# Input read in the transform's own layout, its scale moved into the convolution's kernel, and an inverse stage in eight groups

## The chip, the cores and the metric

The kernel runs on one core of a Trainium2 chip. It has the engines PE (matmul; its weight loads are listed as PEld), DVE, ACT and POOL, and SP, which only issues DMAs here. The metric is the device time of one execution in microseconds; smaller is better. Shares and single durations come from one profiled execution, the times from separate runs.

## The reference

One block of a conditioned state-space layer: a layer norm with shift and scale from a condition vector, a long convolution per channel, a gate and a residual; then a second norm and a two-layer feed-forward part with a squared ReLU. L = 2048 tokens, D = 512 channels, N = 128 states per channel, F = 1792.

```
mod = silu(c) @ w_mod                       # sa, ca, ga, sb, cb, gb, 512 each
h = layernorm(x) * (1 + ca) + sa
K[d, l] = Re sum_n C[d,n] * exp(dt[d] * A[d,n] * l) * dt[d] * B[d,n]
x = x + ga * (causal_conv(h, K) + h * Dskip)
h = layernorm(x) * (1 + cb) + sb
x = x + gb * (relu(h @ w1 + b1)**2 @ w2 + b2)
```

## The kernel before

The convolution is done by a transform of length 2048, split as 32 x 64 (a token is 64 a + b, with b permuted and counted by j), on eight chunks of 64 channels, c = 0 to 7. Partitions hold 32 values of a for each of four groups of 128 channels; along a partition run j and the channels.

**Start.** `parameters` works out the phases and amplitudes of all states from A, B, C and dt on DVE, ACT and POOL, first for chunk 0, then for the other seven. The input x arrives as 16 row blocks `rows` of 128 tokens by 512 channels. For each, DVE takes mean and variance (L527, L528), subtracts the mean and multiplies by the scale (L597), multiplies by the reciprocal deviation and adds the shift (L598); 16 matmuls with columns of the identity turn the block into the transform's layout (L602) and ACT copies it into `big1` (L605). Scale and shift rows `g1`, `s1` come from matmuls of the condition with `w_mod` (L550, L587).

**Main loop**, 32 units u of 16 channels, four to a chunk. For each unit POOL makes phases (`kgen_phase`, L729) and amplitudes (`kgen_amp`, L749, L753), ACT their sine, absolute value and cosine (`kgen_sin`, L739 to L741), DVE the products (`kgen_rl`, L763 to L766), and PE sums over the states into a PSUM bank `kg` (`kgen_mm`, L773); copied to `ksb` (L836), that is a piece of the convolution kernel K. Both K and the input go through `stage1` (L639, copy L641) and `stage2` (L649). For the input the result is kept by ACT (L672), and two DMAs make a copy with its halves exchanged (L676); for the kernel, DVE multiplies stage two's result with both (L783). A matmul back (L792) and two DVE copies (L798) leave each chunk in `big0` and `big1`. Which chunk's pieces are issued behind which unit is written by hand in the string `ORDER`: capitals are the input's pieces (`u_pieces`), small letters the products (`product_pieces`), `x` exponentials (L720), `l` the late modulation, `r` the row pieces. Seven large tiles `xy` are handed round for all of this; one buffer of them holds a stationary operand's source until its last reader is done.

**Inverse stage.** `inverse(n)`, n = 0 to 3, each 128 matmuls of 32x32 by 128 columns (L946), gives four blocks s of 128 tokens each in the four halves of the PSUM tiles `tg`; n = 0 is added to x by DVE (L953), the others are copied by ACT (L955) and added by POOL (L958). `statistics` and `prepare` normalize (L964 to L973), transpose (L979), apply scale and shift (L982, L986) and split each block into a high half (L990, ACT) and a low half (L992, POOL) of reduced-precision numbers. The weights w1 and w2 are split likewise (L897, L918 for w1; `split`, L893, L894, for w2). L975 adds the gated bias b2 to x.

**Feed-forward.** For each of four groups of 512 tokens 14 tiles: `ffn1` (L1040, L1041 on the high half, L1043 on the low) and, two tiles later, `ffn2` (L1060 to L1062).

**What sets the order.** The program is traced, and `keep_order` then lists it anew for every engine: a list scheduler with a cost for each instruction (`weight`), a model of PE's clock, the dependences, and a priority that is the cost to the end plus a number given by `hurry` for single passages. Groups in `in_turn` keep the order of the source. SP's DMAs go by the source's order as they become ready. Each engine then runs its list strictly in order.

## Time and profile before

| | us |
|---|---|
| runs, without the profiler | 654.75, 654.25, 648.11 (median 654.25) |
| the profiled execution's own time | 646.92 |
| its span, first to last instruction | 645.1 |
| start, until stage one of the input begins (L639) | 63.5 |
| main loop, until the first inverse matmul (L946) | 232.1 |
| inverse stage, until ffn2 begins | about 40 |
| feed-forward, from there to the end | about 309 |

The parts are cut at the first instruction named. PE's clock column shows 1.00 of full speed except in the inverse stage, where stretches of 16 us show between 0.68 and 0.89. A line of a group gives busy time, the mean of one instruction and the idle time of its engine before it with what ended it; a matmul in this number format appears as two records.

### The profile page before, as it was taken

The numbers are of one execution on the slowest core, as the hardware profiler recorded it, in microseconds if no ns is written. First come the engines' busy times: TensorE is split into PE (matmuls) and PEld (weight loads), VectorE is DVE, ScalarE is ACT, GpSimd is POOL, SyncE is SP. The second block draws the span as 40 slices with busy tenths as digits, with TensorE's granted clock in tenths as the row PEclk, the third lists the DMA queues.
The fourth block names the chain that finished last, engine by engine and source line by source line (L and its number), as shares of the span: only waits on it lengthen the run. The fifth ranks groups of instructions, "written<-read, shape, count | busy, mean of one in ns | idle before, by whom it ended". The sixth has DMA issues, their size and how long they took to land.

```text
span 645.1 us, 20810 instructions
## 1 busy us (share of the span) xinstructions
PE 584.7 (91%) x9314; PEld 507.1 (79%) x9314; DVE 384.0 (60%) x655; ACT 342.2 (53%) x632; POOL 302.7 (47%) x243
## 2 busy tenths in 40 slices
PE   1367998999899999987899999999999999999995
PEld 1265997899799998885668888888888888888884
DVE  6999956899799778744659532533325333252223
ACT  5963888989887977361645532244322433222220
POOL 5696799889999887158969300011000100000000
PEclk9999999999999999998799999999999999999998
DMA  9942030311331233465222000100001000010001
GB/s 324 381 133 68 3 69 4 68 36 38 69 70 39 82 69 86 139 206 201 85 83 73 28 0 1 65 1 0 1 1 66 1 1 1 0 66 0 1 1 65
DMA packets 21705, 42.30 MB, mean 66 GB/s; under 512 B 3696, under 2 KB 9200, under 8 KB 20336
## 3 DMA queue, kind: packets, MB, share of 16 engines
q1 hardware_dynamic: 21184, 40.84, 20.8%
q8 instruction: 73, 1.20, 0.8%
q10 hardware_dynamic: 432, 0.14, 0.1%
q14 instruction: 16, 0.13, 0.1%
HBM read 28.39 MB, written 4.19 MB: 51 GB/s over the span
## 4 chain that ended last, share of the span: by engine, by line
PE 71%; DVE 11%; POOL 7%; issue 5%; ACT 4%; DMA 2%; DVEq 0%; SPq 0%; POOLq 0%; ACTq 0%
PE tg L1060 8%; PE tg L1062 8%; PE tg L1061 8%; PE ps L1040 6%; PE ps L1041 6%; PE ps L1043 6%; PE ps L649 6%; PE ps L792 6%; PE ps L639 5%; PE kg L773 3%; PE kg L1040 2%; PE kg L1041 2%; PE kg L1043 2%; ACT tables L720 2%; DVE xy L598 2%
## 5 line engine op out<-in xcount | busy, mean ns | idle before, releaser
L1048 DVE TENSOR_TENSOR xy<-xy 128x512 f32<-128x512 f32 x56 | 44.6, 796 | 157.8 <-ACT rw L1047 106.2
L1046 ACT ACTIVATE xy<-ps,b1c 128x512 f32<-128x512 f32 x42 | 28.9, 688 | 129.7 <-PE ps L1043 129.7
L975 POOL TENSOR_TENSOR big<-big,lo 128x512 f32<-128x512 f32 x16 | 21.6, 1355 | 152.9 <-DVE xy L973 152.5
L649 PE MATMUL ps<-xy,t_sb 128*64 128x64 f32 x2048 | 67.1, 223 | 1.8 <-DVE xy L783 0.9
L649 PEld LDWEIGHTS ps<-xy,t_sb 128*64 128x64 f32 x2048 | 63.9, 138 | 3.8 <-issue 1.1
L792 PE MATMUL ps<-e_sb,xy 128*64 128x128 f32 x1024 | 61.3, 274 | 4.7 <-ACT xy L641 1.9
L792 PEld LDWEIGHTS ps<-e_sb,xy 128*64 128x64 f32 x1024 | 56.0, 139 | 6.3 <-ACT xy L641 2.3
L641 ACT COPY xy<-ps 128x512 f32<-128x512 f32 x64 | 36.8, 589 | 11.8 <-PE ps L639 10.1
L753 POOL TENSOR_TENSOR rtl<-tables 128x1024 f32<-128x1024 f32 x22 | 43.0, 1955 | 0.1
L783 DVE TENSOR_TENSOR xy<-ps,xy 128x512 f32<-128x512 f32 x64 | 40.0, 683 | 2.0 <-PE ps L649 1.7
L798 DVE COPY big<-ps 128x256 f32<-128x256 f32 x64 | 24.2, 419 | 20.3 <-PE ps L792 20.0
L729 POOL TENSOR_TENSOR llph<-lo,big 128x1024 int32<-128x1024 int32 x16 | 34.3, 2141 | 3.8 <-ACT tg L741 2.3
L1040 PE MATMUL ps<-h0h,w1h 128*128 128x512 f32 x88 | 35.8, 407 | 0.0
L729 POOL TENSOR_TENSOR rtl<-lo,big 128x1024 int32<-128x1024 int32 x16 | 34.3, 2141 | 2.8 <-ACT tg L741 2.1
L639 PE MATMUL ps<-d_sb,ksb 128*64 128x128 f32 x512 | 33.2, 274 | 1.1 <-DVE ksb L837 0.6
L639 PE MATMUL ps<-d_sb,big 128*64 128x128 f32 x512 | 31.4, 274 | 0.8 <-ACT big L605 0.7
L1040 PE MATMUL ps<-h,w1h 128*128 128x512 f32 x80 | 31.4, 393 | 0.0
L1046 ACT ACTIVATE xy<-kg,b1c 128x512 f32<-128x512 f32 x14 | 9.6, 689 | 39.4 <-PE kg L1043 39.4
L1049 DVE TENSOR_TENSOR rw<-xy,rw 128x512 fp32r<-128x512 f32 x37 | 28.5, 770 | 2.9
L639 PEld LDWEIGHTS ps<-d_sb,ksb 128*64 128x64 f32 x512 | 28.0, 137 | 2.3 <-DVE ksb L837 1.0
L639 PEld LDWEIGHTS ps<-d_sb,big 128*64 128x64 f32 x512 | 27.9, 137 | 2.0 <-ACT big L605 1.0
L773 PE MATMUL kg<-rtl 128*32 128x64 f32 x1408 | 25.6, 221 | 4.1 <-issue 4.1
(247 smaller groups left out, 1574.0 us busy)
## 6 DMA issues: line engine op xcount, KB each, us to landing
xy<-xt SPq DMA_DIRECT2D x32, 256.0 KB, 5.2
xy<-xy SPq DMA_DIRECT2D x16, 512.0 KB, 6.1
xy<-w_mod SPq DMA_DIRECT2D x6, 1024.0 KB, 8.6
out_dram<-xy SPq DMA_DIRECT2D x16, 256.0 KB, 2.1
xy<-w SPq DMA_DIRECT2D x14, 256.0 KB, 2.7
raw<-w SPq DMA_DIRECT2D x6, 512.0 KB, 5.4
t_sb<-c_t SPq DMA_DIRECT2D x1, 2048.0 KB, 16.9
i2c<-c_i SPq DMA_DIRECT2D x1, 2048.0 KB, 8.7
```

Of the source, the lines that this page charges most:

```text
L639: nc.tensor.matmul(ps[64 * r : 64 * r + 64, 128 * i : 128 * i + 128], src[:, i], d1_sb[:, r], start=True, stop=True)
L649: nc.tensor.matmul(ps[64 * r : 64 * r + 64, 64 * i : 64 * i + 64].rearrange("p (h q t) -> p q h t", h=2, t=2), t2_sb[:, 8 * g + i, r], src ...
L729: nc.gpsimd.tensor_tensor(ph.rearrange("p d r (a b) -> p (d r) a b", a=4), bc(low_phase[:, us].rearrange("p d r b -> p (d r) b"), 2, 4), b ...
L773: nc.tensor.matmul(kps[32 * q : 32 * q + 32, d, :], am[:, r, 4 * q + d, 64:96], am[:, r, 4 * q + d, 0:64], start=(r == 0), stop=(r == 1))
L792: nc.tensor.matmul(ps[64 * m : 64 * m + 64, 128 * i : 128 * i + 128], pairs(y)[:, g, i // 2, 64 * m : 64 * m + 64, i % 2], e1_sb[:, h], st ...
L1040: pe.append(nc.tensor.matmul(ps, w1h[:, q, fs], hh[:, q, :], start=(q == 0), stop=False))
L1041: pe.append(nc.tensor.matmul(ps, wl[:, q], hh[:, q, :], start=False, stop=False))
L1043: pe.append(nc.tensor.matmul(ps, w1h[:, q, fs], hl[:, q, :], start=False, stop=(q == 3)))
L1048: nc.vector.tensor_mul(rr, rr, rr)
L1060: pe.append(nc.tensor.matmul(acc, r2l[:, ms], hi_, start=(t == 0), stop=False))
L1061: pe.append(nc.tensor.matmul(acc, r2h[:, ms], lo_, start=False, stop=False))
L1062: pe.append(nc.tensor.matmul(acc, r2h[:, ms], hi_, start=False, stop=(t == NF - 1)))
```

## The change

**Input.** A second copy of x, `xl`, laid out as `big1` needs it, is loaded straight into `big1` by eight DMAs of 512 KB in place of the 16 row blocks. Means and variances of a token now lie across four partitions: 64 `bn_stats` on 128 columns each, two small matmuls with an averaging matrix `avg` for the mean, two for the variance. ACT then scales each of the 64 pieces in place (L590 of the change). L527, L528, L597, L598, L602 and L605 are gone.

**Scale.** The scale 1 + ca, the gate and 1/L are multiplied into the kernel's amplitude factors `wa` (L658) and into Dskip; the shift, divided by the scale, is added by DVE to each chunk just before its stage one (L718). A guard keeps the divisor from zero. Stage one of the input takes its stationary operand from `big1` with the channels innermost: 64 values that are 128 elements apart.

**Loop.** The exchange by DMA is a piece of its own (digits in `ORDER`), the last chunk's products are in `ORDER` too, and the string is new. The bank `kg` holds one unit in place of two, and the shift row beside it. Temporaries of `parameters` lie in PSUM.

**Inverse stage.** Eight groups of 64 matmuls (L994), two token blocks each; the first two are added by DVE (L1003), the second of them in the banks of `tb`; the others are copied by ACT, 256 columns at a time (L1005). For the first four blocks ACT makes the normalization (L1026) and DVE applies three quarters of scale and shift (L1038) in place of two. Adding b2 to these four blocks (L1078) comes behind. The groups n = 0 to 3 keep the source's order.

**Scheduler.** `weight` has other numbers, `keep_order` models PE's instruction fetch by blocks, and the numbers given to `hurry` are others.

Core of the diff:

```diff
 ORDER = (
-    "rxrrrrrrrrrrrrrrrABAAABDAlAA..DBBA.BD.BDaDBaaDaCCa..xaBaaC.C.CbbDbbCEECb."
+    "AAAxAAAABxA.C.ClB.CBB.BB0CaBCaaaBaa.D1..xaa.bDbbDbCCD.C.bD.bFbb.D2cDcccFEccD."
...
+            words = sum(length(i) for i in groups[g])
+            while count + words - done > block:
...
-    zj = [f.rearrange("p (c j d) -> p c j d", c=NC, j=64) for f in flat]
-    x_sb = [flat[1][:, 1024 * c : 1024 * c + 1024].rearrange("p (d j) -> p d j", j=64) for c in range(NC)]
+    zj = [flat[0].rearrange("p (c j d) -> p c j d", c=NC, j=64), flat[1].rearrange("p (j c d) -> p c j d", j=64, c=NC)]
+    xc = [zj[1][:, c] for c in range(NC)]
...
-            nc.sync.dma_start(rows[4 * k + i], xt[4 * k + i])
+    for i in range(8):
+        nc.sync.dma_start(flat[1][:, 1024 * i : 1024 * i + 1024], xl[:, 1024 * i : 1024 * i + 1024])
...
+        for j in range(64)[js]:
+            nc.vector.bn_stats(stj[:, j], flat[1][:, 128 * j : 128 * j + 128])
+            nc.tensor.matmul(mean, avg, groups[:, 1, h], start=(h == 0), stop=(h == 1))
+    hurry(mark, 82139)
+    for j in range(64):
+        xr = flat[1][:, 128 * j : 128 * j + 128]
+        nc.scalar.activation(xr, xr, AF.Identity, scale=rj[:, j : j + 1], bias=nj1[:, j : j + 1])
+    hurry(mark, -122334)
...
-            nc.vector.scalar_tensor_tensor(row, row, mv1[:, s, 0:1], g1, op0=ALU.subtract, op1=ALU.mult)
-            nc.vector.scalar_tensor_tensor(row, row, mv1[:, s, 1:2], s1, op0=ALU.mult, op1=ALU.add)
+    nc.vector.tensor_mul(shift_row, mps[0], c4)
+    nc.vector.tensor_mul(ds4, ds4, g4)
+        nc.vector.tensor_mul(wa, wa, gp.rearrange("p (c x) -> p c x", c=NC)[:, c : c + n])
...
     def u_pieces(c):
+        nc.vector.tensor_add(xc[c], xc[c], bc(shift_row[:, 16 * c : 16 * c + 16], 1, 64))
+        x_sb = xc[c].rearrange("p j d -> p d j")
...
+    def swap_piece(c):
...
     def inverse(n):
-        banks = [t.rearrange("p (i c d) -> p i c d", i=4, c=NC) for t in accs]
+        banks = [t[:, 0:256].rearrange("p (i c d) -> p i c d", i=2, c=NC) for t in (tb if n == 1 else accs)]
+        if n < 4:
+            in_turn.update(whole)
...
+            nc.scalar.activation(d4(xn), x2[:, s], AF.Identity, scale=rstd2[:, s : s + 1], bias=mv[:, s, 1:2])
+        if s > 3:
+            nc.gpsimd.tensor_add(x2[:, s], x2[:, s], d4(b2g))
```

What the new lists look like at three places. **ACT, end of the start.** Names are lines of the kernel that each row is from. Before, behind the last parameter operations (L494 to L496) and among the first unit's sine (`tg`, L739 to L741):

```order
L494 ACTIVATE big_83<-big_83 128x7x64
L495 ACTIVATE big_83<-big_83 128x7x64
L496 ACTIVATE big_83<-big_83,halfpi 128x7x64
L739 ACTIVATE tg_416<-rtl 128x1024
L740 ACTIVATE rtl<-rtl 128x1024
L605 COPY big_84<-ps_151 128x128x4
L741 ACTIVATE tg_417<-rtl,halfpi 128x1024
```

In the change, the same operations (now L524 to L526 and L794 to L796), the scalings L590 and the first copy of stage one (L691):

```order
L590 ACTIVATE big_86<-big_86,nj_73,rj 128x128 x7
L524 ACTIVATE big_85<-big_85 128x7x64
L525 ACTIVATE big_85<-big_85 128x7x64
L526 ACTIVATE big_85<-big_85,halfpi 128x7x64
L794 ACTIVATE tg_153<-rtl 128x1024
L795 ACTIVATE rtl<-rtl 128x1024
L796 ACTIVATE tg_154<-rtl,halfpi 128x1024
L643 ACTIVATE g_456<-xy_93,tiny 128x128
L644 ACTIVATE xy_93<-xy_93 128x128
L590 ACTIVATE big_86<-big_86,nj_73,rj 128x128 x47
L691 COPY xy_99<-ps_145 128x512
L794 ACTIVATE tg_153<-llph 128x1024
```

The copies L605 are gone, and 47 of the 64 scalings stand between the first unit's cosine and the second unit's sine.

**DVE, start of the loop.** Before, the end of the row arithmetic, parameter work of chunks 1 to 7 (`big`, L473, L502) and the first unit's products:

```order
L597 SCALAR_TENSOR_TENSOR xy_94<-xy_94,mv_71,kg_351 128x512
L598 SCALAR_TENSOR_TENSOR xy_94<-xy_94,mv_71,ps_150 128x512
L473 TENSOR_SCALAR big_83<-big_83 128x7x64
L502 TENSOR_SCALAR big_83<-big_83 128x7x64 x2
L763 SCALAR_TENSOR_TENSOR rtl<-rtl,tg_416 128x16x32
L764 TENSOR_TENSOR rtl<-rtl,tg_416 128x16x64
L502 TENSOR_SCALAR big_83<-big_83 128x7x128 x2
L765 TENSOR_TENSOR rtl<-rtl,tg_417 128x16x32
L766 TENSOR_TENSOR rtl<-rtl,tg_417 128x16x64
```

In the change, the amplitude factors (L658), the shift of two chunks (L718), the rest of the first unit's products (L819, L821) and the second unit's:

```order
L658 TENSOR_TENSOR big_85<-big_85,ps_144 128x64
L658 TENSOR_TENSOR big_85<-big_85,ps_144 128x7x64
L718 TENSOR_TENSOR big_86<-big_86,kg_152 128x64x16 x2
L819 TENSOR_TENSOR rtl<-rtl,tg_153 128x16x64
L821 TENSOR_TENSOR rtl<-rtl,tg_154 128x16x64
L818 SCALAR_TENSOR_TENSOR rtl<-rtl,tg_153 128x16x32
```

The parameter work has moved ahead of this place, and the first two shifts stand ahead of two of the first unit's four products.

**POOL, inverse stage.** Before, the last splits of w1 (L918) and the first of w2 (L894), b2 (L975), x (L958) and the low halves (L992):

```order
L918 TENSOR_TENSOR w1lb<-raw_4469,w1h 128x4x128
L894 TENSOR_TENSOR w_4995<-xy_93,w_4995 128x512
L894 TENSOR_TENSOR w_5005<-xy_93,w_5005 128x512 x3
L975 TENSOR_TENSOR big_83<-big_83,lo 128x4x8x16 x4
L992 TENSOR_TENSOR h0l<-xy_91,h0h 128x4x128
L958 TENSOR_TENSOR big_83<-big_83,xy_92 128x4x8x16 x3
L992 TENSOR_TENSOR h0l<-xy_91,h0h 128x4x128 x3
```

In the change (L966 and L944 are the splits, L1076 the gate times b2, L1078 b2, L1008 x, L1048 the low halves):

```order
L966 TENSOR_TENSOR w1lb<-raw_4352,w1h 128x4x128
L1076 TENSOR_TENSOR lo<-lo 128x512
L944 TENSOR_TENSOR w_5106<-xy_93,w_5106 128x512
L1078 TENSOR_TENSOR big_85<-big_85,lo 128x4x8x16
L944 TENSOR_TENSOR w_5106<-xy_93,w_5106 128x512
L1078 TENSOR_TENSOR big_85<-big_85,lo 128x4x8x16
L1008 TENSOR_TENSOR big_85<-big_85,xy_94 128x4x8x16 x2
L1048 TENSOR_TENSOR h0l<-xy_96,h0h 128x4x128
L1008 TENSOR_TENSOR big_85<-big_85,xy_94 128x4x8x16
L1048 TENSOR_TENSOR h0l<-xy_96,h0h 128x4x128 x3
```

Two of four L975 and one split of w2 stand behind the low halves now; the gate times b2 stood further up before (L890).

More of the change, by code (lines that the diff above doesn't have):

```diff
@@ L590, in tile_adaln_ssm_ffn @@
[L590 to L609 removed]
+    g4, t4 = (ctile(n, [P, 128]) for n in ("g4", "t4"))
```

245 lines of the change are left out of this document (143 added, 102 removed).

## The prediction

> **What bounds the kernel now.** I read busy times by stretches of the span first, then the chain, and only then single rows.
>
> ```profile
> 63.50:295.60 232.10, 219.39 (x6250) 207.94 (x6251) 182.93 (x298) 181.17 (x286) 189.92 (x135) 1.00 0.29 75
> 295.60:320.50 24.90, 18.20 (x785) 13.77 (x785) 14.57 (x36) 11.23 (x27) 22.51 (x17) 0.73 0.33 105
> 320.50:336.20 15.70, 14.67 (x297) 10.90 (x295) 7.98 (x21) 7.48 (x18) 9.99 (x8) 0.89 0.34 102
> 336.20:640.00 303.80, 302.26 (x1356) 249.94 (x1354) 120.67 (x174) 102.18 (x182) 33.98 (x23) 1.00 0.05 16
> ...
> 96.00:172.00 76.00, 69.37 (x2016) 65.02 (x2007) 63.67 (x104) 69.04 (x127) 70.93 (x54) 1.00 0.20 45
> 172.00:282.00 110.00, 107.04 (x3099) 102.52 (x3096) 87.22 (x144) 79.61 (x113) 77.59 (x55) 1.00 0.32 83
> ```
>
> The columns after the stretch are its length and then busy time (instructions) of PE, PEld, DVE, ACT, POOL, then granted clock and DMA. Four parts: a start up to 63.5 us in which PE does little; the main loop to 295.6 us, PE busy 219 of 232 us; the inverse stage to about 336 us at a lowered clock; the feed-forward part, 302 of 304 us on PE. The change leaves the last part's matmuls alone, so it is decided in the first 336 us. The last two rows are pieces of the loop.
>
> How full is PE really in the loop? Busy time counts latency, so I use the pace at which groups follow each other, from the chain (start, length, what):
>
> ```profile
> 212.37 3.49 PE ps L639 x64
> 215.86 1.75 PE ps L792 x32
> 217.61 1.05 PE kg L773 x64
> 218.66 1.02 PE ps L639 x16
> 219.69 0.93 PE ps L649 x32
> ```
>
> and the counts, from the page's groups:
>
> ```profile
> L649 PE MATMUL ps<-xy,t_sb 128*64 128x64 f32 x2048 | 67.1, 223 | 1.8 <-DVE xy L783 0.9
> ...
> L792 PE MATMUL ps<-e_sb,xy 128*64 128x128 f32 x1024 | 61.3, 274 | 4.7 <-ACT xy L641 1.9
> ...
> L639 PE MATMUL ps<-d_sb,ksb 128*64 128x128 f32 x512 | 33.2, 274 | 1.1 <-DVE ksb L837 0.6
> ...
> L639 PE MATMUL ps<-d_sb,big 128*64 128x128 f32 x512 | 31.4, 274 | 0.8 <-ACT big L605 0.7
> ```
>
> Stage two: 64 groups of 32 records at 0.93 = 59.5 us. Transform back (L792): 32 groups at 1.75 = 56.0. Stage one: 64 groups of 16 at 3.49/4 = 0.87, 56.0. Kernel generation (L773): 32 units at 1.05, and the group behind one starts 0.15 late (1.02 against 0.87): 38.4. Late modulation (three groups like L550's, further down) and a broadcast some 3.6. Together 213.5 us of the 232.1: PE is the bound, and **all waits of the loop together are 18.6 us**. No order of the same matmuls can win more there.
>
> **The start.** What lets PE in at 63.5 us is DVE's row arithmetic, 32 wide instructions without a pause:
>
> ```profile
> 38.30 1.41 DVE L597 SCALAR_TENSOR_TENSOR xy<-xy,mv,kg 128x512 f32<-128x512 f32 x2 [0.19 <-PE kg L587]
> ...
> 60.85 0.75 DVE L598 SCALAR_TENSOR_TENSOR xy<-xy,mv,ps 128x512 f32<-128x512 f32 x1
> 63.52 6.62 PE L639 MATMUL ps<-d_sb,big 128*64 128x128 f32 x112 [0.69 <-ACT big L605]
> ```
>
> The change removes these 23 us, the 512 records of transposing matmuls and their 16 copies. In their place ACT scales 64 pieces of 128x128 (new L590), and no chunk's stage one can begin before the last. So the gate moves to ACT's queue, summed from these rows:
>
> ```profile
> 8.23 0.58 ACT L442 COPY big<-ps 128x512 f32<-128x512 f32 x1 [1.84 <-PE ps L439]
> ...
> 9.28 3.67 ACT L720 ACTIVATE tables<-big 128x64 f32<-128x64 f32 x24 [0.47 <-POOL big L458]
> 13.95 9.06 ACT L720 ACTIVATE tables<-big 128x64 f32<-128x64 f32 x48
> ...
> 24.98 1.28 ACT L529 ACT_TABLE_LOAD   x1
> ...
> 38.15 0.58 ACT L494 ACTIVATE big<-big 128x448 f32<-128x448 int32 x1 [2.93 <-DVE big L491]
> ...
> 41.59 1.03 ACT L739 ACTIVATE tg<-rtl 128x1024 f32<-128x1024 int32 x1 [1.70 <-POOL rtl L729]
> ...
> 422.89 1.50 ACT L986 ACTIVATE xy<-kg,sbc,cbc 128x128 f32<-128x128 f32 x4 [1.81 <-PE kg L979]
> ```
>
> Before the last L590 stand 72 exponentials (12.6), three table loads (3.8), twelve parameter operations on 448 columns (about 0.58 each, 7.0) and twelve on 64 (at the exponentials' 0.15 or somewhat more, 2.9), one unit's sine, absolute value and cosine (each near L739's 1.03, 3.2), L442 and small ones (1.2) and 64 scalings. L986 is the nearest row for these: 128x128 with a scale and a bias from memory; four take 1.50 with the last one's 0.46 in it, so they follow each other at 0.35: 22.2 us. Sum 52.9; from L442's start at 8.2 us that is 61.1, with 0.7 for waits on POOL 61.8. DVE then adds the shift to the chunks (new L718, 1024 elements, one operand in PSUM; L764 below has that size, 1.21), one before the first stage one: it starts near 63.2, against 63.5: **-0.3 us**. The ends: pieces that overlap no more than a single L986 row (0.46) put 7 us on it; pieces at the exponentials' 128-wide pace, (9.06 - 3.6)/24 = 0.23, take 7.5 off. I keep 0.35, its row being the same form.
>
> ```profile
> 13.42 1.86 DVE L527 BATCH_NORM_STATS2 st<-xy 128x6 f32<-128x512 f32 x3
> ...
> 64.13 1.21 DVE L764 TENSOR_TENSOR rtl<-rtl,tg 128x1024 f32<-128x1024 f32 x1
> ```
>
> The statistics cost nothing there: 64 of 128 elements, at a quarter to a half of L527's 0.6 us each 10 to 19 us on DVE from about 10 us, done by 29 at worst, while L590 can't begin before ACT's third table load at about 31. The load has the same 4 MB.
>
> **The first microseconds of the loop.** Before, PE has been busy with transposes since 40.8 us; now it comes from idleness. A row early and one late, the same 32 records:
>
> ```profile
> 22.49 1.94 PE L550 MATMUL ps<-xy,srep 128*32 128x128 f32 x32 [14.30 <-DVE mv L528]
> ...
> 74.46 1.08 PE L550 MATMUL ps<-xy,srep 128*32 128x128 f32 x32 [0.32 <-DVE sbc L626]
> ```
>
> After idleness the work runs at about half pace, though the clock column shows 1.00 there. So the four stage-one groups that now come first take up to 7.0 us in place of 3.5. [...]
>
> Behind them ACT's fourth stage-one copy stands behind the sine of the third unit, which waits for DVE's products of the second, and these for the two shifts: at about 71 us, where before seven groups were done by 70. The two delays lie partly under one another. I take **+4 us**, between 3 and 6.
>
> **The rest of the loop.** The waits:
>
> ```profile
> 171.05 0.43 PE L773 MATMUL kg<-rtl 128*32 128x64 f32 x13 [1.97 <-issue]
> ...
> 287.83 7.21 PE L792 MATMUL ps<-e_sb,xy 128*64 128x128 f32 x128 [1.92 <-DVE xy L783]
> ...
> 73.16 4.28 POOL L501 TENSOR_TENSOR big<-big 128x896 int32<-128x896 int32 x2
> 77.40 1.07 POOL L749 TENSOR_TENSOR rtl<-tables 128x512 f32<-128x512 f32 x1
> ```
>
> By the two pieces quoted first, PE has 6.6 us of gaps from 96 to 172 us and 3.0 in the 110 us after; in the earlier one POOL, busy 71 of 76, makes the kernel's amplitudes one unit after another without a pause. In the change POOL's last parameter work (three like the 2.14 of L501 here, 6.4 us from 66 us on) is done during ACT's scalings; its rows up to the fourth unit's amplitudes are otherwise the same, so these start at about 71 us, against 77.4 here. So it leads by some 6 us, and waits that come from it can go. DVE gets 8 shifts, 9.7 us: it is busy 183 of 232, and they hide there unless one delays a product. The new order spreads the exchange DMAs and the last chunk's product: that chunk's 1.92 us wait has a broadcast matmul group put into it. Issue stalls (1.97 here) I leave in part. Of 18.6 us I take 9 to stay: **-9.6 us**; the ends are nothing and -14.
>
> **The inverse stage.** Eight groups of half the size let the first two rows' statistics start 2.5 us sooner, and move a normalization from DVE to ACT. But the first feed-forward tile needs the low halves, which POOL makes:
>
> ```profile
> 281.09 2.38 POOL L918 TENSOR_TENSOR w1la<-raw,w1h 128x1024 fp32r<-128x1024 f32 x1 [20.98 <-PE ps L792]
> ...
> 308.70 5.47 POOL L975 TENSOR_TENSOR big<-big,lo 128x512 f32<-128x512 f32 x4
> 319.06 3.96 POOL L992 TENSOR_TENSOR h0l<-xy,h0h 128x512 fp32r<-128x512 f32 x3
> ...
> 323.59 1.49 PE L1043 MATMUL ps<-h0l,w1h 128*128 128x512 f32 x4
> ```
>
> From 281.1 to 323.0 POOL needs 41.9 us, and L1043 follows at 323.6, 28.0 after the loop's end. In the change two of four L975 and one split of a w2 block move behind: -2.7 - 1.3 (a POOL operation on 512 elements each, as in these rows), about 37.9, of which some 2 were waits. But it starts when the seventh chunk's last L792 frees a buffer, and behind that now come only two stage-two groups, a broadcast, the products' wait and four L792: 1.9 + 0.6 + 1.1 + 7.0 = 10.6 before the end, against 14.5. So the low halves land 25.5 to 27.5 us behind it, against 27.4: **-1 us**. Ends: -5, if the clock recovers sooner, and +2, if ACT's 24 half-size evictions, in place of 12, hold up the high halves.
>
> **Sum**: -0.3 + 4 - 9.6 - 1 = -6.9 us on the profiled execution, 646.92 us (645.1 of span): 640. Two runs of three lie at 654.5, one at 648.1, and no row says why; I carry the difference to the mean of all four executions, 651.0, and predict **644**.
>
> **Rivals.** *Nothing is won* (0.20): the loop keeps 14 of its waits behind a slow start, or a scaling takes 0.40: -0.3 + 4 - 4 - 1 = -1, about 650. For it: PE has only 3 us of gaps from 172 to 282 us as it is. Against: POOL's lead. *More is won* (0.17): waits down to the ends, inverse stage too: -0.3 + 3 - 14 - 5 = -16, 635.
>
> *Slower: the stationary operand is read with a stride* (0.13). Stage one of the input took 64 neighbouring columns of big; now it takes every 128th element. Loads hide under matmuls today:
>
> ```profile
> L639 PEld LDWEIGHTS ps<-d_sb,big 128*64 128x64 f32 x512 | 27.9, 137 | 2.0 <-ACT big L605 1.0
> ...
> L1040 PEld LDWEIGHTS ps<-h,w1h 128*128 128x128 f32 x80 | 15.0, 188 | 3.0
> ```
>
> 64 columns more cost 50 ns, and a record is issued every 55 ns, so a load at half its pace, 100 ns, would set the pace: 512 x 45 ns = 23 us, all on PE in the loop: -6.9 + 23 = +16, 667. It decides from a load about a tenth slower than now. Against it: L649's moving operand reads 16-byte pieces at such a stride at 29 ns per 64 columns, no slower than L639's 55 per 128 neighbours; no row shows single elements. [...]
>
> **How the numbers follow.** The forecast, 638 to 650, has 0.50; four in five of it lie over 1% below 651 (about what a measurement of this kernel can tell from no change). With "more" that makes 0.55 faster; the rest of the forecast and most of "nothing" 0.27 within; the stride and a bad start 0.18 slower. From 632 to 657 the range holds all but the stride and the tails.
>
> **What would show it.** Right: last L590 near 62 us, first stage one near 63 us, the row work gone; loop end near 290; waits in it 9 and 4; feed-forward as long as before. Wrong: loads over 150 ns in stage one of the input, scalings over 0.4 us apart, or loop waits as before.

## The result and the profile after

The changed kernel takes **656.73 us** (median of 20 runs, 649.42 to 663.44) against 652.12 us before (median of 20, 647.63 to 654.99). The ratio is 1.0062, 95% interval 1.0038 to 1.0086: slower by 0.6%, where 644 us had been forecast. The ratio leaves out five of the change's runs, 659.88 us and longer, which count as slow. The profiled execution of the change took 649.42 us, the shortest of its 20 runs; its span is 647.6 us. A second profile of the unaltered change (experiment 3) took 656.49 us and stands beside it:

| us, from PE's rows | before | change | change, second profile |
|---|---|---|---|
| first stage one of the input | 63.5 | 68.8 | 68.4 |
| loop, to the first inverse matmul | 232.1 | 232.7 | 236.2 |
| from there to the first ffn2 matmul | 40.2 | 37.0 | 41.0 |
| from there to the end | 309.3 | 309.2 | 309.2 |
| span | 645.1 | 647.6 | 654.7 |

The same stretches as before, read by windows of the change (length, then busy time and instructions of PE, PEld, DVE, ACT, POOL, granted clock, DMA share and GB/s):

```profile
68.76:301.50 232.74, 228.73 (x6250) 220.10 (x6251) 187.25 (x299) 184.11 (x286) 183.67 (x133) 0.99 0.29 77
301.50:324.90 23.40, 17.72 (x784) 13.17 (x784) 18.16 (x47) 13.75 (x36) 23.35 (x18) 0.76 0.37 97
324.90:338.50 13.60, 13.60 (x296) 10.57 (x294) 9.57 (x23) 7.94 (x24) 13.28 (x11) 0.91 0.42 118
338.50:640.00 301.50, 301.50 (x1354) 249.52 (x1353) 113.55 (x166) 101.12 (x178) 31.39 (x22) 1.00 0.05 16
```

The loop has the length that it had, with the same number of PE instructions, yet PE is busy for 228.7 us of it and was for 219.4. So PE's idle time in the loop went from 12.7 us to 4.0, as forecast, and something filled it. The groups of PE's loads and two pieces of the chain say what:

```profile
L689 PEld LDWEIGHTS ps<-d_sb,big 128*64 128x64 f32 x512 | 41.9, 248 | 9.8 <-DVE big L718 8.6 <-DVE mt L673 0.6
L689 PEld LDWEIGHTS ps<-d_sb,ksb 128*64 128x64 f32 x512 | 28.6, 138 | 0.9 <-issue 0.2
```

```profile
129.56 1.23 PE ps L689 x16
...
269.04 1.02 PE ps L689 x16
```

L689 is stage one. With the input as stationary operand (`big`, 128 elements apart) a load takes 248 ns, before 137, and 16 records take 1.23 us. With the kernel's piece (`ksb`, neighbours) a load takes 138 ns, and even a group that pays for starting behind another shape (second row) takes 1.02. That is the third rival of the prediction, at a smaller price.

The start, in ACT's and PE's rows:

```profile
27.50 0.31 ACT L582 ACTIVATE rj<-ps,epsb 128x64 f32<-128x64 f32 x1 [2.19 <-PE ps L581]
...
45.44 1.03 ACT L794 ACTIVATE tg<-rtl 128x1024 f32<-128x1024 int32 x1 [1.14 <-POOL rtl L784]
...
49.28 18.18 ACT L590 ACTIVATE big<-big,nj,rj 128x128 f32<-128x128 f32 x47
...
68.77 6.73 PE L689 MATMUL ps<-d_sb,big 128*64 128x128 f32 x64 [8.34 <-DVE big L718]
```

47 scalings in 18.18 us follow each other at 0.387 us, and ACT waits 3.3 us for PE and POOL on the way. So the last scaling ends at 67.5 and not at 61.8. And POOL, which was to be 6 us early with the fourth unit's amplitudes (L804), waits for ACT's cosine:

```profile
75.09 2.15 POOL L784 TENSOR_TENSOR llph<-lo,big 128x1024 int32<-128x1024 int32 x1 [3.88 <-ACT tg L796]
77.19 1.08 POOL L804 TENSOR_TENSOR rtl<-tables 128x512 f32<-128x512 f32 x1
```

### The profile page after: what moved, and what is told of

Its sections match the earlier page's. It is cut to its first block, busy times and chain, and to the rows that moved or that the text cites. A ratio compares the mean times of both kernels' runs of the same rounds, so it can differ in the third digit from the quotient of the medians.

```text
span 647.6 us, 19866 instructions
## 1 busy us (share of the span) xinstructions
PE 573.0 (88%) x8802; PEld 503.0 (78%) x8802; DVE 381.6 (59%) x686; ACT 363.4 (56%) x695; POOL 300.2 (46%) x243
## 4 chain that ended last, share of the span: by engine, by line
PE 81%; ACT 7%; DVE 5%; issue 2%; POOL 2%; DMA 1%; DVEq 0%; SPq 0%; POOLq 0%; ACTq 0%
PE ps L689 10%; PE ps L699 8%; PE tg L1124 8%; PE tg L1122 8%; PE tg L1123 8%; PE ps L847 7%; PE ps L1102 6%; PE ps L1103 6%; PE ps L1105 6%; PE kg L828 5%; ACT big L590 3%; PE kg L1102 2%; PE kg L1103 2%; PE kg L1105 2%; DVE xy L571 2%
## 5 line engine op out<-in xcount | busy, mean ns | idle before, releaser
L1110 DVE TENSOR_TENSOR xy<-xy 128x512 f32<-128x512 f32 x56 | 42.6, 760 | 159.6 <-ACT rw L1109 106.6
L1031 POOL TENSOR_TENSOR big<-big,lo 128x512 f32<-128x512 f32 x12 | 15.7, 1306 | 153.9 <-DVE xy L1028 153.9
L847 PE MATMUL ps<-e_sb,xy 128*64 128x128 f32 x1024 | 60.5, 273 | 0.3 <-DVE xy L838 0.3
L847 PEld LDWEIGHTS ps<-e_sb,xy 128*64 128x64 f32 x1024 | 56.3, 139 | 1.1 <-DVE xy L838 0.5
L689 PE MATMUL ps<-d_sb,big 128*64 128x128 f32 x512 | 45.5, 328 | 8.7 <-DVE big L718 8.3
L691 ACT COPY xy<-ps 128x512 f32<-128x512 f32 x64 | 37.3, 593 | 22.0 <-PE ps L689 21.7
L689 PEld LDWEIGHTS ps<-d_sb,big 128*64 128x64 f32 x512 | 41.9, 248 | 9.8 <-DVE big L718 8.6
L838 DVE TENSOR_TENSOR xy<-ps,xy 128x512 f32<-128x512 f32 x64 | 40.2, 684 | 4.7 <-PE ps L699 4.3
L784 POOL TENSOR_TENSOR llph<-lo,big 128x1024 int32<-128x1024 int32 x16 | 34.5, 2155 | 11.8 <-ACT tg L796 9.3
L689 PE MATMUL ps<-d_sb,ksb 128*64 128x128 f32 x512 | 33.8, 274 | 0.0
L689 PEld LDWEIGHTS ps<-d_sb,ksb 128*64 128x64 f32 x512 | 28.6, 138 | 0.9 <-issue 0.2
L804 POOL TENSOR_TENSOR rtl<-tables 128x512 f32<-128x512 f32 x22 | 23.6, 1077 | 11.0 <-PE kg L828 9.9
## 6 DMA issues: line engine op xcount, KB each, us to landing
xy<-w_mod SPq DMA_DIRECT2D x6, 1024.0 KB, 12.7
```

What stands on the lines that cost most here:

```text
L689: nc.tensor.matmul(ps[64 * r : 64 * r + 64, 128 * i : 128 * i + 128], src[:, i], d1_sb[:, r], start=True, stop=True)
L784: nc.gpsimd.tensor_tensor(ph.rearrange("p d r (a b) -> p (d r) a b", a=4), bc(low_phase[:, us].rearrange("p d r b -> p (d r) b"), 2, 4), b ...
L847: nc.tensor.matmul(ps[64 * m : 64 * m + 64, 128 * i : 128 * i + 128], pairs(y)[:, g, i // 2, 64 * m : 64 * m + 64, i % 2], e1_sb[:, h], st ...
L1110: nc.vector.tensor_mul(rr, rr, rr)
```

## Experiments

Ratios are to the kernel before, timed on the same chip. "Kept order" means that every instruction stands on its engine as in the changed kernel. `...` in a diff or a view marks what is left out. PE's idle time in a loop is its length less PE's busy time.

### 1. The distance between the elements of a stationary operand

**Before, with the distance alone.** The order on all engines is that of the kernel before.

```diff
-    z4 = [[f[:, 1024 * c : 1024 * c + 1024].rearrange("p (j d) -> p j d", j=64) for c in range(NC)] for f in flat]
-    zj = [f.rearrange("p (c j d) -> p c j d", c=NC, j=64) for f in flat]
-    x_sb = [flat[1][:, 1024 * c : 1024 * c + 1024].rearrange("p (d j) -> p d j", j=64) for c in range(NC)]
-    xj = flat[1].rearrange("p (d j) -> p d j", j=64)
+    zj = [flat[0].rearrange("p (c j d) -> p c j d", c=NC, j=64), flat[1].rearrange("p (j c d) -> p c j d", j=64, c=NC)]
+    z4 = [[z[:, c] for c in range(NC)] for z in zj]
+    x_sb = [z.rearrange("p j d -> p d j") for z in z4[1]]
+    xj = flat[1].rearrange("p (j d) -> p d j", j=64)
```

> The kernel before, in its own order, with one thing changed: the input of stage one lies with the rows outermost, so that the 64 elements of a stationary operand are 128 elements (512 bytes) apart and not neighbours. Theory A (the distance makes the weight load slow): a group of 16 records of stage one of the input takes about 1.23 us and not 0.87, a load about 248 ns and not 137; 32 groups make 11.5 us, of which some falls into waits that the loop has anyway, so 4 to 11.5 us longer, ratio 1.006 to 1.018. Theory B (the loads are slow in the changed kernel because its loop is fuller or its clock was low): load 137 ns, 0.87 us a group, ratio 1.000 within 0.003.

658.06 us, ratio 1.0111 (1.0076 to 1.0147). The loads' group, and PE's first rows of stage one (before: 112 records in 6.62 us):

```profile
L639 PEld LDWEIGHTS ps<-d_sb,big 128*64 128x64 f32 x512 | 39.3, 251 | 1.8 <-ACT big L605 1.4
...
64.57 8.56 PE L639 MATMUL ps<-d_sb,big 128*64 128x128 f32 x112 [1.17 <-ACT big L605]
```

Seven groups in 8.56 us are 1.22 each. By PE's rows the 32 input groups took 39.0 us in place of 29.2, and the loop 243.9 in place of 232.1: all of the 9.8 us, and 2 more, reached the loop's end. Between the medians of the runs lie 8.0 us. A side effect of the edit stands outside the loop: ACT's copies into the new layout (L605) take 1.09 us each and not 0.58, and the start is 1.1 us later. Theory A holds and B falls. The change pays this too: by the same rows its 32 input groups take 41.9 us, with about 2 us of half clock (granted 0.50) in the first of them (experiment 2).

**The change, with 1, 4 and 16 elements' distance.** The input is laid out by channels, so that the 64 elements lie 1, 4 or 16 apart. No row's statistics can begin before the whole input has landed, and the scheduler makes another order. From the run with 4:

```diff
-    xc = [zj[1][:, c] for c in range(NC)]
+    xg = flat[1].rearrange("p (g j e) -> p g e j", j=64, e=4)
...
-            nc.vector.bn_stats(stj[:, j], flat[1][:, 128 * j : 128 * j + 128])
+            nc.vector.bn_stats(stj[:, j], xg[:, :, :, j])
...
+        x_sb = [xg[:, (16 * c + d) // 4, d % 4] for d in range(16)]
...
-        "xl": x.transpose(2, 0, 1, 3).reshape(128, 8192),
+        "xl": x.transpose(2, 0, 1, 3).reshape(128, 64, 32, 4).transpose(0, 2, 1, 3).reshape(128, 8192),
```

> The changed kernel with the input loaded channels outermost, so that the 64 elements of a stationary operand of stage one are neighbours again; the rest as in the change. A: load 137 ns, 0.87 us a group; the loop from the first stage one to the first matmul of the inverse falls from 232.7 us to between 221 and 227. The start may be up to 4 us later, since no row's statistics can begin before the whole input has landed. Time 646 to 653 us, ratio to the kernel before 0.985 to 1.000. B: 1.23 us a group as in the change, loop near 232, time 657 or more.

> As the run with neighbours, but with the 64 elements 4 elements (16 bytes) apart. [...]

> As the run before, with the 64 elements 16 elements (64 bytes) apart. [...] By distance: somewhere between 139 and 248 ns, or still 139 if the step comes above 64 bytes.

With neighbours 671.32 us, ratio 1.0315 (1.026 to 1.0371); with 4 and 16 one execution each, 665.75 and 660.91. As times these are misses: with neighbours the scalings have a distance of 64 elements themselves and take 0.53 us each (46 in 24.42), the statistics start at 19.3 us in place of 10.0, and stage one begins at 88.8. With 4 and 16 it begins at 75.1 and 75.3. With neighbours the loop takes 232.6 us and not 221 to 227, as PE stands idle for 9.8 us of it in the new order. As measurements of a load the three are clean, and other runs fit in (247 to 251 ns for the 512 loads at 128, 205 and 206 at 16, up to 150 for neighbours; only the 64 loads that stay at 128 in the run with seven eighths near took 198):

| distance, elements of 4 bytes | 1 | 2 (L847 in the change) | 4 | 16 | 128 |
|---|---|---|---|---|---|
| mean load, ns | 137 to 150 | 139 | 209 | 205 to 206 | 247 to 251 |

```profile
L689 PEld LDWEIGHTS ps<-d_sb,big 128*64 128x64 f32 x512 | 35.3, 209 | 10.0 <-DVE big L718 8.2 <-DVE mt L673 0.6 <-ACT xy L691 0.6
```

One step lies between 8 and 16 bytes (139 to 209 ns), another between 64 and 512 (205 or 206 to 247 and more); from 16 to 64 bytes the price does not rise (209, then 205 to 206). What makes the two steps no run shows.

**The change in its kept order, seven eighths of the distance gone.**

```diff
-ps[64 * r : 64 * r + 64, 128 * i : 128 * i + 128], src[:, i], d1_sb[:, r], start=True, stop=True)
+ps[64 * r : 64 * r + 64, 128 * i : 128 * i + 128], src[:, i] if i + r == 0 or 'big' not in src.tensor.name else ident[:, 0:64], d1_sb[:, r], start=True, stop=True)
```

> The changed kernel in its own order on every engine, but of the eight matmuls of a stage-one group of the input only the first reads the input (128 elements apart); the other seven read 64 neighbouring elements of a constant tile, so seven eighths of the input's transform are left out of the result. Nothing else moves. A (distance): a group takes 0.95 us and not 1.23 to 1.3, 9 us less on PE over 32 groups; if PE sets the loop, it falls from 232.7 us to 224 to 226 and the time by 7 to 9 us, to 647 to 650, ratio 0.993 to 0.999. C (other engines set the loop): the loop falls by less than 3 us, waits of PE grow from 4 to over 10 us, ratio 1.002 to 1.008.

650.82 us, ratio 1.0013 (0.9976 to 1.0051): lower than the change by about 0.5%, between the ranges of A and C. The two intervals overlap a little. As the order is the same here but for three operations that stand somewhat earlier (L675, L676, L796), rows can be set side by side. Amplitude rows on POOL (L804) and products on DVE (L838) come earlier (minus) or later than in the first profile of the change by (us):

| at, in the change | L804, 85.4 | L804, 169.3 | L804, 248.2 | L838, 274.7 | L838, 286.9 |
|---|---|---|---|---|---|
| seven eighths near | -0.7 | -4.8 | -5.8 | -5.8 | -2.1 |
| 16 apart, rows loaded | +1.8 | -0.8 | -1.9 | -1.9 | +1.6 |
| half of the scalings | -4.4 | +2.1 | +2.4 | +2.4 | +4.9 |
| the same, one DVE operation less | -4.3 | -4.9 | -4.9 | -4.9 | -0.8 |
| both | -4.5 | -9.2 | -9.9 | -9.9 | -4.2 |
| useless matmuls, kept order | +3.3 | +3.6 | +6.0 | +7.1 | +10.0 |
| the change again | -0.2 | -0.2 | -0.2 | -0.2 | +3.3 |

PE's input groups take 32.7 us and not 41.9. Of these 9 us PE passes 5.8 on by 248 us; the rest turns into waits. What is lost from 275 us on is lost by the change itself in its second profile. Nine of the ten profiles in this order lose 2.5 to 5.7 us between the last two columns against the first profile of the change, whose execution was the shortest of 20; so the last column is better read against the row of the change again. At that place of the program, 14 records into a group of L828, the chains read, first this run:

```profile
269.78 0.37 PE kg L828 x14
270.15 1.97 issue
272.12 0.94 PE kg L828 x49
```

and the change, first profile:

```profile
275.61 0.37 PE kg L828 x14
275.97 0.61 issue
276.58 0.94 PE kg L828 x49
```

PE stands with no releaser in both, for 0.6 or 2.0 us. Experiment 3 takes this up.

**The change in its kept order, 16 elements' distance.**

```diff
-    zj = [flat[0].rearrange("p (c j d) -> p c j d", c=NC, j=64), flat[1].rearrange("p (j c d) -> p c j d", j=64, c=NC)]
+    zj = [f.rearrange("p (c j d) -> p c j d", c=NC, j=64) for f in flat]
...
-        nc.sync.dma_start(flat[1][:, 1024 * i : 1024 * i + 1024], xl[:, 1024 * i : 1024 * i + 1024])
+        nc.sync.dma_start(zj[1][:, :, 8 * i : 8 * i + 8].rearrange("p c j d -> p c (j d)"), xl[:, 1024 * i : 1024 * i + 1024].rearrange("p (c x) -> p c x", c=NC))
```

> The changed kernel in its own order on every engine, with the input in the order chunk, row, channel: the 64 elements of a stationary operand are 16 elements (64 bytes) apart and no longer 128; loaded by rows in pieces of 512 bytes, so that the statistics can start as early as in the change. By the loads at 16 apart (206 ns, about 1.0 us a group) 6 to 7 us less on PE. A: time lower by 4 to 7 us than the changed kernel, 650 to 653, ratio 0.997 to 1.003; C: within 2 us of it, 655 to 658. If the pieces of 512 bytes land late, the first stage one is later than 68.8 us and eats the gain.

653.26 us, ratio 1.0076 (1.0046 to 1.0107): no gain in time. The start is 2.1 us later: the statistics wait for the loads, whose issue in pieces of 512 bytes took SP 15.8 us and not 8.7. By 248 us the loop has won 3.7 (from +1.8 to -1.9), less than the 6.7 us that PE's input groups save (35.2 and not 41.9). The time is above A's range.

### 2. The order and the start

**The change with the scheduler's old table of durations.** Only the order differs.

```diff
-                return 26, 26 + 250
-            if getattr(ins, "is_transpose", False):
-                return 88, 88 + 170
+                return 42, 42 + 200
...
-            t = 250 + 1.72 * n
+            t = 180 + 1.72 * n
```

> The changed kernel with one thing put back: the planner's table of how long an instruction takes, as it was before. The instructions are the same, only their order on the engines differs. Theory: the short waits of the changed loop (4 us) come from an order that fits just this program, so another order of the same work lengthens the loop from 232.7 us to 242 to 255, waits of PE 12 to 20 us, ratio 1.015 to 1.035. Rival: they come from what the change does (statistics, scalings and shifts in place of rows and transposes), so the loop stays within 3 us of 232.7, ratio 1.003 to 1.009.

671.8 us, ratio 1.0322 (1.0264 to 1.038). The loop takes 247.7 us, 15 more, while the start is the same (68.4). PE is idle for 14.0 us of it and not 4.0. The longest waits in it (total, times, longest):

```profile
PE ps L681 <- ACT xy L683: 4.3, 2, 3.5
PE kg L820 <- issue: 2.5, 2, 2.0
PE ps L839 <- ACT xy L683: 1.1, 1, 1.1
PE kg L820 <- DVE ksb L884: 1.1, 1, 1.1
```

(Lines are 8 lower here: L681 is stage one.) So statistics, scalings and shifts alone do not make short waits: with the same instructions in another order they are about as long as before the change. Whether an order tuned by the old table (`ORDER`, `hurry`) would also have had short ones was not tried.

**Four runs with another order and something else.** In the first two the shift is made for four channels at a time, in the second of them in place, as a control:

```diff
-        nc.vector.tensor_add(xc[c], xc[c], bc(shift_row[:, 16 * c : 16 * c + 16], 1, 64))
...
+            xg = xc[c].rearrange("p j d -> p d j")[:, 4 * g : 4 * g + 4]
+            nc.vector.tensor_add(near4[g % 2], xg, bc(shift_row[:, 16 * c + 4 * g : 16 * c + 4 * g + 4], 2, 64))
+            stage1(near4[g % 2], xs, 4 * g)
```

> The changed kernel, with the shift made by channel groups (32 additions of 256 elements in place of 8 of 1024), each written into one of two small buffers in which the 64 elements of a stationary operand are neighbours; load, statistics and scalings as in the change. A (distance): a group of stage one of the input 0.91 us and not 1.23, loads 137 ns; if PE sets the loop, it falls from 232.7 us to 221 to 224, and the time to 645 to 649, ratio 0.985 to 0.995. Rival C (PE did not set the loop in the changed kernel; the products and amplitudes on DVE and POOL did): loop stays at 230 or more, the waits of PE grow from 4 to about 14 us, ratio 1.000 to 1.010.

> The control of the run before: the shift by channel groups, but written in place, so that the stationary operand stays 128 elements apart. A: 1.23 us a group and a time as the changed kernel's, ratio 1.002 to 1.010; against the run with the buffers some 8 to 10 us longer. C: as long as the run with the buffers, within 2 us.

Then every second scaling on DVE, and useless matmuls ahead of the loop (both edits also put the new instructions ahead of others):

```diff
+        (nc.vector.tensor_scalar(xr, xr, rj[:, j : j + 1], nj1[:, j : j + 1], op0=ALU.mult, op1=ALU.add) if j % 2 else nc.scalar.activation(xr, xr, AF.Identity, scale=rj[:, j : j + 1], bias=nj1[:, j : j + 1]))
```

```diff
+    warm = bank("ps", PS)
+    [nc.tensor.matmul(warm[0:64, 0:128], d1_sb[:, 0, 0:64], zj[1][:, 7, j : j + 8], start=True, stop=True) for j, n in ((40, 16), (48, 16), (56, 10)) for _ in range(n)]
```

> The changed kernel with every second of the 64 scalings on DVE, ahead of its work on the parameters. Theory of the start: ACT's queue is the gate, so 32 scalings of 0.386 us less open the first stage one about 12 us earlier, near 57 us, or near 60 if DVE's chain to the shift row becomes the gate; the loop then waits for POOL's amplitudes part of that, so the time falls by 4 to 10 us, 647 to 653, ratio 0.990 to 1.000. Rival: POOL's work on the parameters sets when kernels come, the loop gets as much longer as the start gets shorter, 655 to 658.

> The changed kernel with 42 matmuls of no use put on PE ahead of the first stage one, each set of them waiting for eight scaled rows, so that PE is busy from about 61 us. If idleness before costs the pace, the first 64 records take 4.6 to 5.2 us and not 6.7, and the time falls by 2 to 4 us, to 653 to 655; if the pace of the first group has another cause, or the loop waits for something else at its start, 6.7 us or no change of the time, 656 to 658.

667.58, 671.43, 664.16 and 668.94 us; ratios 1.0296 (1.0198 to 1.0394), 1.0324 (1.0244 to 1.0404), 1.0227 (1.0144 to 1.031) and 1.0296 (1.0214 to 1.0378). All missed, and alike: the scheduler made a new order from each edit, with PE idle in the loop for 19.8, 19.4, 22.1 and 14.8 us against 4.0, and loops of 247 to 258 us. Between the first two, whose loads took 150 and 248 ns, lie 3.9 us and not 8 to 10, each in an order of its own. In the third the start did move, to 55.5 us, and the loop took 258.0. The fourth tells nothing of idleness, as the scheduler put the scalings that the useless matmuls wait for first, so that these were over by 58.1 us and PE idle again. These four say only that an edit here is measured with its order, and led to the kept order.

**Useless matmuls, kept order** (the fourth edit, written to the bank `gp`).

> The changed kernel with 42 matmuls of no use ahead of the first stage one, each set of them behind eight more scaled rows, and every other instruction in the order of the changed kernel. If idleness costs the pace, the first 64 records take 4.6 to 5.4 us and not 6.7. If that start is on the path to the end, the time falls by 1.5 to 3 us (ratio lower by 0.002 to 0.005 than the changed kernel's 1.006); if the loop's start waits for kernels anyway, no change.

658.91 us, ratio 1.0137 (1.0103 to 1.017). PE's rows:

```profile
60.99 11.82 PE L660 MATMUL ps<-big,d_sb 128*64 128x128 f32 x83 [0.92 <-ACT big L590]
72.55 0.38 PE L689 MATMUL ps<-d_sb,big 128*64 128x128 f32 x1
...
72.76 4.74 PE L689 MATMUL ps<-d_sb,big 128*64 128x128 f32 x63
```

The useless work took 11.8 us, so stage one began 3.8 us late. But its first 64 records then took 4.95 us from the first start to the last end, against 6.73. In windows of 4 us the change's granted clock is 0.50 from 66 to 74 us; here it is 0.50, 0.72, and 1.00 from 68 on. Idleness costs 1.8 us there. No gain of time shows, as stage one itself begins later for it.

**Half of the scalings, kept order**, and then the same with one operation less on DVE.

```diff
-    for j in range(64):
+    for j in range(0, 64, 2):
```

> The changed kernel in its own order, with every second of the 64 scalings left out (half of the rows go unscaled into the transform). Theory of the start: the first stage one comes 6 us earlier, near 62.5 us, since DVE's products of amplitudes and gate at 61.2 us become the gate; PE's work passes the gain on, and the time falls by 4 to 6 us, to 651 to 653, ratio 0.998 to 1.002. Rival: kernel amplitudes set the loop's first part, PE waits for them, and the time falls by less than 2 us, ratio 1.003 to 1.008.

652.72 us, ratio 1.0038 (1.0007 to 1.0068). Stage one begins at 62.0, 6.7 us earlier, and the gain is gone by 105 us. DVE's row at that place, and then POOL's beside it:

```profile
89.34 6.93 DVE L677 TENSOR_SCALAR cbc<-cbc 128x4 f32<-128x4 f32 x1
```

```profile
89.06 2.15 POOL L784 TENSOR_TENSOR rtl<-lo,big 128x1024 int32<-128x1024 int32 x1
91.16 1.08 POOL L804 TENSOR_TENSOR rtl<-tables 128x512 f32<-128x512 f32 x1
92.18 1.97 POOL L808 TENSOR_TENSOR rtl<-tables 128x1024 f32<-128x1024 f32 x1
94.09 2.15 POOL L784 TENSOR_TENSOR llph<-lo,big 128x1024 int32<-128x1024 int32 x1
```

Adding 1 to four numbers per partition took 6.93 us, to the end of POOL's unbroken run, and PE waited 5.4 us for the copy behind it. The same row took 0.20 us in the run with seven eighths near, where it began just ahead of an operation of POOL, and 1.37 in the change.

```diff
-        nc.vector.tensor_scalar_add(cbc, cbc, 1.0)
+            (nc.vector.tensor_scalar_add if v is cbc else nc.vector.tensor_copy)(v, tp[:, 0:128].rearrange("p (q a) -> p q a", q=4)[:, :, 0], *((1.0,) if v is cbc else ()))
```

> As the run with half of the scalings left out, with one operation less on DVE: the addition to the 128x4 modulation vector, which took 6.93 us there while POOL worked on without a pause, is made in the copy from PSUM before it. If that wait gave the start's gain back, the loop keeps 4 to 5 us of the 6.7, the time is 4 to 6 us below the changed kernel's, ratio 0.996 to 1.001. If PE waits for something else by 110 us, as long as with half the scalings alone, ratio 1.002 to 1.006.

649.69 us, ratio 1.0026 (0.9982 to 1.007): the time moved less than the interval. But in the table above the lead of 4.9 us now stands to 275 us, and only there it is lost. The wait was the cause of the loss by 105 us, and 4.9 of the start's 6.7 us are passed on to 275 us.

**Both** (the run before, and seven eighths of the loads from neighbours as well).

> The run before together with seven of eight stationary operands of the input replaced by neighbours (half of the scalings and seven eighths of the input's transform are left out of the result). If start and stride are both on the path, the gains add: 5 and 4 to 9 us, ratio 0.985 to 0.995. If PE is then held by late instructions or kernels, not more than the better of the two alone, ratio 0.995 to 1.001.

644.45 us, ratio 0.9916 (0.988 to 0.9952). The leads add to 9.9 us by 248 us; at 287 us 4.2 are left against the first profile and 7.5 against the second. Start and distance are both on the path to the end, and with most of both left out the change is faster than the kernel before.

### 3. From 275 us on

**The change again.**

> The changed kernel once more, unaltered, for the profile of another execution: the one profiled took 649.4 us, the median of its runs 656.7. If the difference is instructions that arrive late on PE, the start (68.8 us) and the feed-forward part (309.15 us from the first second-layer matmul's end of the inverse on) stay, and the loop and the inverse stage together are 5 to 8 us longer with 5 us more of waits that name no releaser; if it is the start, the first stage one is 5 us later; if it is the clock, the feed-forward part is longer.

656.49 us. Up to 275 us its rows agree with the first profile within 0.3. Then the two waits without a releaser in L828 come to 3.9 us (0.6 there), and the inverse stage, to the first ffn1, takes 27.7 us and not 23.4. Pieces of its chain, windows of 4 us, and a DVE row of the inverse stage:

```profile
275.44 0.37 PE kg L828 x14
275.80 1.98 issue
```

```profile
268.00:272.00 4.00, 4.00 (x143) 3.91 (x133) 3.68 (x6) 2.50 (x5) 0.12 (x1) 1.00 0.57 150
272.00:276.00 4.00, 3.80 (x132) 3.57 (x129) 3.49 (x7) 0.94 (x2) 0.00 (x0) 1.00 0.97 304
```

```profile
316.26 5.44 DVE L1024 SCALAR_TENSOR_TENSOR mv<-mv,rstd 128x1 f32<-128x1 f32 x1
```

The first of the two waits stands behind record 14 of that group in nine of the ten profiles of this order. It begins at the end of 4 us in which loads fill the DMA engines (share 0.97). But in the first profile the share is 0.93 there and the wait 0.6 us, and the second wait here falls at 0.53. What PE waits for no row names, and its cause stays open. The second item is new with the change: L1024 makes the bias of a normalization on ACT, one number per partition, while POOL works without a pause. In the first profile that row took 0.40 us; in the second it ended with POOL's unbroken run, at 321.7 us. Over 16 profiles with the change's inverse stage one of its four rows took 3.8 to 5.6 us in six, and those inverse stages took 26.1 to 30.0 us; the others 23.4 to 26.2.

**The change without both short operations on DVE, kept order.**

```diff
-            nc.vector.scalar_tensor_tensor(
-                mv[:, s, 1:2], mv[:, s, 0:1], -1.0, rstd2[:, s : s + 1], op0=ALU.mult, op1=ALU.mult)
+            nc.scalar.activation(mv[:, s, 0:1], mv[:, s, 0:1], AF.Identity, scale=-1.0)
+            nc.scalar.activation(mv[:, s, 1:2], mv[:, s, 0:1], AF.Identity, scale=rstd2[:, s : s + 1])
```

> The changed kernel in its own order, with the two DVE operations of 1 and 4 elements that can stand still beside POOL's work taken away from there: the bias of the first four normalizations (L1024, 128x1, 0.16 to 5.6 us in the runs so far) is made by two short operations on ACT, the 1 is added to the modulation vector in the copy from PSUM. Theory: L1024's long cases are the 4 us by which the inverse stage differs from run to run, so this kernel's inverse stage takes 23 to 25 us always, and the median falls by 2 to 4 us below the changed kernel's: ratio 0.999 to 1.003. If the spread comes from late instructions alone, ratio 1.004 to 1.008.

653.07 us, ratio 1.0039 (1.0008 to 1.0071), just above the upper end expected. The inverse stage took 24.3 us in a profile whose loop lost 5.1 us by 287 us. The interval overlaps the change's own, so it is likely, and not shown, that these operations make some 2 us of the median.

**The parts together:** this, the load of the run with 16 apart, and ten scalings on POOL (kept order otherwise).

```diff
+        (nc.gpsimd.tensor_scalar(xr, xr, rj[:, j : j + 1], nj1[:, j : j + 1], op0=ALU.mult, op1=ALU.add) if j >= 54 else nc.scalar.activation(xr, xr, AF.Identity, scale=rj[:, j : j + 1], bias=nj1[:, j : j + 1]))
```

> The run before, with the input in the order chunk, row, channel (64 elements 64 bytes apart and not 512) and the last ten of the 64 scalings on POOL, which has nothing to do from 27 to 34 us. Expected by the parts: 5 us less on PE in the loop by 270 us, the start 2 us later by the load in pieces of 512 bytes and 3.5 us earlier by the ten scalings, 2 to 4 us less in the inverse stage, of which late instructions may take 3 back: ratio 0.988 to 0.998. If the scalings on POOL take over 0.6 us each, POOL's later work and the loop's start slip by 2 us and more, ratio 0.998 to 1.004.

646.25 us (643.98 to 651.42, 12 runs), ratio **0.9944** (0.9916 to 0.9972): faster than both kernels. Its loop and inverse stage:

```profile
67.22:297.06 229.84, 221.33 (x6250) 212.31 (x6251) 185.12 (x298) 181.68 (x286) 186.20 (x134) 0.99 0.29 78
297.06:321.16 24.10, 18.84 (x784) 14.04 (x784) 15.02 (x43) 14.86 (x44) 24.02 (x19) 0.72 0.33 94
```

```profile
31.01 4.31 POOL L590 TENSOR_SCALAR big<-big,rj,nj 128x128 f32<-128x128 f32 x10 [1.54 <-DVE nj L584]
```

Ten scalings take 4.31 us on an idle POOL. The start is 1.6 us earlier, the loop 2.9 us shorter than in the change's first profile.

## Why the prediction was wrong

**The step that failed** is the cost of loading the input's stationary operand at a distance of 128 elements. The sum has no term for it. The prediction saw the mechanism, gave it 0.13 as a rival, and set it aside by a comparison with L649's moving operand, which is read in 16-byte pieces; such pieces say nothing on single elements. The runs show a load of 248 to 251 ns in place of 137, 9.8 us more on PE by the distance alone, and a loop 11.8 us longer (the kernel before with the distance alone). The rest of the difference is the start, whose term was mis-sized.

| us, on the profiled executions | forecast | first profile |
|---|---|---|
| start | -0.3 | +5.3 |
| first microseconds of the loop | +4 | +1.8, the half clock (granted 0.50) |
| loads at a distance | none | +9.8 to +10.9 |
| rest of the loop (what remains of its +0.6) | -9.6 | -11.0 to -12.1 |
| inverse stage, to the first ffn2 | -1 | -3.3 |
| sum, with -0.1 of the feed-forward part | -6.9 | +2.5 |

Differences are taken before rounding. The two values for the loads are the kernel before with the distance alone, and the change's own rows (41.9 less 29.2 us, less the half clock).

- **Start.** The scaling's pace was taken as 0.35 us, from four rows that read PSUM (L986), where rows from `big` measured 0.387. That is 2.4 us over 64. Waits of ACT, taken as 0.7, were 3.3. When 6.7 us of the start were given back, 4.9 reached 275 us: about three quarters of this term count.
- **First microseconds of the loop.** The half pace was right (granted clock 0.50 from 66 to 74 us), its price was not: 6.73 us against 4.95 for the same records with PE kept busy, where up to 7.0 against 3.5 had been counted. The delay of products behind the shifts was not measured by itself.
- **Loads at a distance.** The rival was priced at 23 us, more than twice what it cost: a load became 1.8 times as long, but a group only 1.34 times (1.22 against 0.91), and a record grew by 19 ns where its load grew by 114: most of a load lies under the matmuls.
- **Rest of the loop.** That the waits would fall was right, and too timid: PE's idle time fell from 12.7 to 4.0 us. Its ground was wrong. POOL's lead of 6 us did not exist: the fourth unit's amplitudes (L804) began at 77.2 us, before at 77.4, after POOL had idled 3.9 us for ACT's cosine. The same instructions in another order have 14.0 us of idle time and a loop 15 us longer, so it is this order that holds the waits down.
- **The loop's balance.** No gain at all is what is left: 8.7 us less of idle time and 9.3 more of work. In the other direction the work is not fully worth its time: of 9 us taken from PE in the kept order 5.8 remained at 248 us.
- **Inverse stage.** To the first ffn2 it is 3.3 us shorter in the first profile and 0.7 longer in the second. Where that gain is lost, the prediction did not look: the small operation L1024 that the change adds on DVE, and POOL beside it.

The first profile is the shortest of 20 executions, and so the +2.5 is less than the 4.6 us between the medians. The second profile shows where 7 us more can go: 3.4 in the loop, 4.0 to the first ffn2.

Of the three signs named as wrong, loads over 150 ns came true (248); scalings over 0.4 us apart did not, though 0.387 was enough; waits did not stay as before.

## What to carry to other kernels

When a change alters a layout, look at every operand that is read with the new distance, the stationary one too, and price it by a row with that distance or by both ends, not by an operand of another kind that happens to be strided. In a program whose order comes from a scheduler, hold the order fixed when a part is tested: the useless matmuls took 668.94 us in a new order and 658.91 in the kept one. Count the tiny operations that a change adds: one that makes four numbers per partition stood 6.93 us beside POOL, longer than any single operation of POOL there.

## What was not expected of the hardware

The same small DVE operation took very different times: L677 on 128x4 between 0.20 and 6.93 us, L1024 on 128x1 between 0.16 and 5.6. In the second profile of the change L1024 took 5.44 us while POOL worked, and 0.16 just after POOL's run had ended at 321.7 us. The 6.93 us are longer than any one of POOL's operations there (2.15), and the row ended with the fourth of them. In the change the same row, L677, took 1.37 us and ended with the POOL operation during which it began, though POOL went on; no row says what decides. The scheduler adds no wait for POOL to operations of up to four elements.

Groups of 512 loads of 64 elements have three prices by distance, 137 to 150, 205 to 209 and 247 to 251 ns; at 16 and 64 bytes the price is nearly the same (209, 205 to 206). And SP took 15.8 us to issue 4 MB in pieces of 512 bytes, 8.7 us in pieces of 4 KB, with the DMA engines busy meanwhile in both (share 0.99 for the larger pieces, 0.9 or more for the smaller).
